# Steps 12 to 15 of a fused attention and network kernel worked in pairs, and two loads moved from one queue to another

## The chip, the cores and the metric

The kernel runs on one core of a Trainium2 chip. The metric is the device time of one execution in microseconds (us): the median over several runs. A core has four compute engines that the text names as the profile does: PE (the tensor engine: matmuls and transposes; its weight loads are shown apart as PEld), DVE (vector), ACT (scalar) and POOL (GpSimd). SP only issues transfers. All five take their instructions strictly in the order in which they were written for them, and wait for one another by semaphores. SBUF is the on-chip memory, PSUM the eight banks into which PE writes its results.

## The reference

```python
# attention, 4 batches x 8 heads, 768 positions, head size 64
k_sum = blocks of 32 keys, largest;  v_sum = blocks of 32 values, mean
scores_l = scale * q @ k.T, kept where |i - j| < 16
scores_s = scale * q @ k_sum.T + log(32)
a = softmax of [scores_l, scores_s];  attn = a @ [v, v_sum]
# network on the 3072 tokens, d_model 512, d_ff 1024
x = attn, heads side by side
out = (((x @ w1) * (x @ w2)) @ w3) @ w_out
```

## The kernel before, in words

**Work.** The 3072 tokens are six units of 512 (`U`), the eight heads four pairs of heads (`NPAIR`). One attention *step* is one unit and one pair: 24 steps, numbered unit by unit, so that steps 12 to 15 are the unit 3. A step has three pieces on PE: the scores (`scores`, L376, 32 small matmuls into two banks of the four called `sc`), the transposes of the softmax (`transposes`, L434, 16 into two banks) and the outputs (`outputs`, L457, 32 into one bank). Between them DVE takes minima and subtracts (`reduce`, L390), ACT exponentiates (`expose`, L404), ACT and DVE invert, ACT normalizes (`normalize`, L414), ACT, or ACT and DVE, copy the transposes out (`evacuate`, L442 to L446), and ACT copies the outputs (`keep_raw`, L477).

The network takes nearly all of PE. Weights and activations are held as a high and a low part, so each product is three matmuls of 512 columns. `w3` is first folded into `w_out` (`fold_weights`), then units 0 and 1 go the plain way (`gate`, `project`, all at L125), and units 2 with 3 and 4 with 5 go as two large products of seven partial products each (`lanes`, L740; the weights of the seven are sums that were stored to DRAM and are loaded back as `ws`). The first large product needs all outputs of units 2 and 3, that is of steps 8 to 15; its operands `xT` are made from them by `moving_x`.

**The written order.** The order on PE is written by hand. The network's matmuls are a generator, `stream`; `run(columns)` takes matmuls from it until so many columns have been given, and between two such runs the attention pieces are placed. A matmul is 512 columns, and `FAST` is 12288 columns, 24 matmuls, one partial product over four lanes. In FASTs, the fold ends at 8, the plain unit 0 at 20, the plain unit 1 at 32 (this point is `CLASSIC`), and the start of the large products follows there; `TO_SLOTS`, where the steps from 8 on begin, is 19.52. I call each place where attention pieces stand in the stream an *interruption*.

**Single steps.** Steps 8 to 15 (up to `SINGLE`, four units of four) are placed by `lump` (L1293): transposes of step p-2 and scores of step p, then 18 matmuls, then outputs of step p-2, then matmuls up to `UP_TO[p]`, 1.56 FAST a step. Each lump also loads and reduces two pieces of the later batches (`load_batch`, `reduce_batch`: block maxima of keys and means of values), and `EXTRA` hangs other work on a lump.

**Pairs of steps.** From step 16 on `two_steps` (L1331) places two at a time: the outputs of the pair before last and the scores of this pair, half a `LEAD` of 18 matmuls twice, then the rest of the period given by `BEGINS`, and in its middle the transposes of the pair before (`turn`). The first pair (m = 8) has to finish the single steps 14 and 15. In the written order ACT and DVE follow the same calls (`tc.manual_schedule(engines=VECTOR)`), while copies of the network float between them by priority. `LATER` hangs loads and the making of `xT` on a pair.

**Queues.** POOL's instructions are in written order too: it copies the block maxima into k (`gather`, L363) and issues the transfers of `load_values` (v, L325) from unit 4 on and of `load_scores` (q, L341, and k, L343) from step 18 on. SP issues the rest: v, q and k of earlier steps, the means (`fetch_means`, L359), the weight sums `wS<-sp` (L685) and their way back `ws<-wS` (L785), and the four loads of each of the two joined output weights (`load_joined`, L949, the transfer at L959: `wr<-pR`, 1 MB each half). SP's order past TO_SLOTS is chosen by the scheduler. The tiles `sp` and `ws` come from one set of six buffers, tag `x`, given out in turn; so do q and k (two each), v (two) and the tag `pt` (four, for the copies g and o of the plain units and for the first joined half).

**Banks.** Accumulators of the plain units take two `mm` banks, and every third of unit 1 takes one of the `sc` banks (`bank`, L492).

## Time and profile before

| | |
|---|---|
| runs | 507.43, 504.39, 507.6 us; median 507.43 |
| the profiled execution | 508.66 us, its span 506.9 us |
| PE busy in the span | 483.1 us, 95% |
| DVE, ACT, POOL busy | 357.0, 316.6, 66.5 us |
| granted clock of PE | 1.000 |

The span runs from the first to the last instruction; 1.76 us of the profiled execution lie around it. A line of a group names the source line, the engine, the operation, the tiles written and read, and the count; after the bar its busy time, the mean time of one in ns, and the idle time of the engine ahead of it with what ended it. In a chain of waits each line is a start, a length and what held the end back at that time. "xN" counts instructions. Matmuls overlap, so that one that lasts 390 ns is followed by the next after some 227 ns.

### The profile page before, as it was taken

What the parts mean: (1) busy time and instruction counts of PE and PEld (TensorE: products, weight loads), DVE (VectorE), ACT (ScalarE), POOL (GpSimd) and SP (SyncE); (2) the same over time, 40 slices, a digit from 0 to 9 for tenths busy, and PEclk for the clock granted to TensorE, in tenths of its full rate; (3) what the DMA queues carried; (4) which work ended last, traced back from release to release, by engine and by line L of the source; (5) the groups of instructions that cost most, each with busy time, mean ns of one, the idle gap of its engine ahead of it and who ended that gap; (6) DMA issues with size and microseconds to landing.
All of it is one profiled execution on the core that took longest, in us unless ns stands there. A gap on an engine that the chain in (4) does not pass through costs nothing.

```text
span 506.9 us, 10543 instructions
## 1 busy us (share of the span) xinstructions
PE 483.1 (95%) x3804; PEld 391.0 (77%) x3804; DVE 357.0 (70%) x873; ACT 316.6 (62%) x882; POOL 66.5 (13%) x121
## 2 busy tenths in 40 slices
PE   0889999999999999999997999999999999999997
PEld 0667777788877877777776888878888888888886
DVE  4978886897704888985657895799968029129972
ACT  5589964677716878878894868579634421523710
POOL 1024523000212110100221132112000000000000
PEclk9999999999999999999999999999999999999999
DMA  8998596999499999889999989998868765656762
GB/s 341 410 411 286 209 357 235 372 400 411 148 301 273 264 277 286 256 261 329 343 311 305 331 286 344 316 300 246 233 183 281 227 191 190 203 178 197 212 193 93
DMA packets 56068, 139.29 MB, mean 275 GB/s; under 512 B 6224, under 2 KB 19280, under 8 KB 53456
## 3 DMA queue, kind: packets, MB, share of 16 engines
q1 hardware_dynamic: 51600, 127.44, 74.5%
q0 software_dynamic: 3264, 9.08, 7.3%
q10 hardware_dynamic: 1152, 2.10, 1.1%
q8 instruction: 30, 0.49, 0.4%
q14 instruction: 22, 0.18, 0.1%
HBM read 105.89 MB, written 32.70 MB: 273 GB/s over the span
## 4 chain that ended last, share of the span: by engine, by line
PE 73%; DMA 13%; DVE 6%; ACT 5%; issue 1%; SPq 1%; POOL 0%; POOLq 0%; DVEq 0%; ACTq 0%
PE ln L740 39%; PE mm L125 25%; PE sc L376 4%; PE po L457 3%; DMA k<-in_kW_dram 3%; DMA ws<-wS 3%; DMA v<-in_vW_dram 2%; DMA wS<-sp 2%; PE tp L434 2%; ACT sm L404 2%; DVE w L121 2%; DVE wf L206 1%; DMA vS<-vs 1%; DMA wraw<-in_w_dram 1%; ACT w L220 1%; DMA wraw<-in_wo_dram 1%
## 5 line engine op out<-in xcount | busy, mean ns | idle before, releaser
L740 PE MATMUL ln<-xT,ws 128*128 128x512 f32 x672 | 155.6, 391 | 3.2 <-DMA ws<-wS 3.2
L740 PEld LDWEIGHTS ln<-xT,ws 128*128 128x128 f32 x672 | 125.4, 188 | 30.4 <-DVE xT L121 3.5
L125 PE MATMUL mm<-x,w 128*128 128x512 f32 x384 | 90.8, 394 | 0.2 <-DVE g L531 0.2
L125 PEld LDWEIGHTS mm<-x,w 128*128 128x128 f32 x384 | 71.1, 188 | 16.4 <-issue 0.8
L404 ACT ACTIVATE sm<-sm,mx 128x120 f32<-128x120 f32 x192 | 73.6, 387 | 13.3 <-DVE mx L390 13.1
L740 PE MATMUL ln<-hT,ws 128*128 128x512 f32 (+1 forms) x348 | 77.3, 383 | 0.0
L760 DVE TENSOR_TENSOR tmp<-ln,tmp 128x512 f32<-128x512 f32 (+1 forms) x53 | 35.6, 678 | 54.1 <-PE ln L740 39.3
L740 PEld LDWEIGHTS ln<-hT,ws 128*128 128x128 f32 x348 | 63.7, 188 | 12.8
L125 PE MATMUL mm<-w,w 128*128 128x512 f32 x192 | 49.9, 409 | 15.1 <-ACT w L220 12.5
L643 ACT CAST hT<-hr 128x512 fp32r<-128x512 f32 x56 | 32.1, 628 | 39.3 <-DVE hr L817 30.5
L125 PEld LDWEIGHTS mm<-w,w 128*128 128x128 f32 x192 | 36.0, 193 | 25.9 <-ACT w L220 13.2
L390 DVE CUSTOM_DVE_ANT_0 sm<-sc,mask_sb 128x120 f32<-128x120 f32 x192 | 41.3, 276 | 15.9 <-PE sc L376 15.9
L125 PE MATMUL mm<-wp,h 128*128 128x512 f32 x192 | 46.3, 395 | 0.0
L125 PEld LDWEIGHTS mm<-wp,h 128*128 128x128 f32 x192 | 35.4, 188 | 8.4 <-issue 0.5
L414 ACT ACTIVATE sm<-sm,mx 128x120 f32<-128x120 f32 x128 | 38.8, 388 | 3.1 <-DVE mx L410 2.4
L121 DVE TENSOR_TENSOR hT<-hr,hT 128x512 fp32r<-128x512 f32 x56 | 35.7, 688 | 3.1 <-ACT hT L643 3.0
L404 ACT ACTIVATION_READ_ACCUMULATOR sm<-sm,mx 128x1 f32 x192 | 36.6, 190 | 0.0
L363 POOL COPY k<-ks 128x96 f32<-128x96 f32 (+1 forms) x32 | 14.8, 476 | 157.0 <-DMA k<-in_kW_dram 140.6
L121 DVE TENSOR_TENSOR w<-wf,w 128x1024 fp32r<-128x1024 f32 (+1 forms) x22 | 25.6, 1167 | 8.2 <-ACT w L220 8.2
L220 ACT CAST w<-wf 128x1024 fp32r<-128x1024 f32 (+1 forms) x22 | 21.3, 969 | 14.5 <-DVE wf L206 13.2
L176 ACT ACTIVATE wf<-wraw 128x1024 f32<-128x1024 f32 (+1 forms) x22 | 23.1, 1061 | 7.4 <-DMA wraw<-in_wo_dram 3.8
L376 PE MATMUL sc<-k,q 64*64 64x120 f32 x768 | 25.4, 268 | 1.6 <-issue 0.8
(72 smaller groups left out, 564.0 us busy)
## 6 DMA issues: line engine op xcount, KB each, us to landing
ws<-wS SPq DMA_DIRECT2D x56, 512.0 KB
wraw<-in_w3T_dram SPq DMA_DIRECT2D x8, 1024.0 KB
wraw<-in_w_dram SPq DMA_DIRECT2D x8, 1024.0 KB
wS<-sp SPq DMA_DIRECT2D x16, 512.0 KB
ws<-pS SPq DMA_DIRECT2D x16, 512.0 KB
raw<-in_kT_dram SPq DMA_DIRECT2D x16, 392.0 KB
wS<-w SPq DMA_DIRECT2D x12, 512.0 KB
ws<-pW SPq DMA_DIRECT2D x24, 256.0 KB
```

Source lines behind the costliest of these rows:

```text
L121: eng.tensor_tensor(dst, src, hi.bitcast(F32), ALU.subtract)
L125: nc.tensor.matmul(acc, lhsT=a, rhs=b, start=first and i == 0, stop=last and i == len(terms) - 1)
L176: nc.scalar.activation(f[:, some], words[:, some, 1].bitcast(F32), AF.Prelu, scale=2.0**-112, alpha=-(2.0**32),)
L220: nc.scalar.copy(t[:, 0, some], f[:, some])
L376: nc.tensor.matmul(sc[h][64 * g : 64 * g + 64, i * KR : (i + 1) * KR], lhsT=q[rows, i * P + 64 * g : i * P + 64 * g + 64], rhs=k[rows, i, ...
L390: nc.vector.tensor_tensor_reduce(out=sm[:, j], in0=sc[h][:, i * KR : (i + 1) * KR], in1=mask_sb[:, 0 if blk == 0 else 2 if blk == BLOCKS - ...
L404: nc.scalar.activation(sm[:, j], sm[:, j], AF.Exp, bias=mx[:, 0, j : j + 1], scale=-1.0, accum_out=mx[:, 1, j : j + 1])
L414: nc.scalar.activation(sm[:, j], sm[:, j], AF.Copy, scale=mx[:, 2, j : j + 1])
L457: nc.tensor.matmul(po[cols, at : at + 64], lhsT=v[:KR, g, i, cols], rhs=pt[g][:, (h * NBLK + i) * 64 : (h * NBLK + i + 1) * 64], start=Tru ...
L643: nc.scalar.copy(dst[0], src)
L740: nc.tensor.matmul(bank[:, cols], lhsT=x, rhs=y[:, cols], start=c + j == 0 and (split or k in o.first), stop=c == steps - 1 and j == 2 and ...
L760: nc.vector.tensor_tensor(parts[to][:, cols], got, parts[more][:, cols], ALU.add)
```

## The change

Eight things change. (1) `LAST_UNITS` goes from 4 to 3, so single steps end with step 11 and pairs begin with m = 6; steps 12 to 15 are the pairs m = 6 and 7. `BEGINS` gets two entries more and a new third: the pairs begin at 25.3, 28.1, 31, 36, 40, 43.7, 46.2 and 50.6 FAST, and the four single steps left have 1.445 FAST each. (2) What the first pair had to do for the single steps is now done at m = 6 for steps 10 and 11. (3) Pairs 6 and 7 (`ahead`) also reduce and load the later batches, twice each, and pair 7 copies the second halves of its transposes out on DVE. (4) In the pair m = 8 (`BLOCKED`) the outputs of steps 14 and 15 aren't left to the next pair: they are placed at 33.4 FAST (`LAST_OUTPUTS`), the transposes before them at 32.4; their v is fetched at the pair's start. (5) Work of `EXTRA` for lumps 13 to 15 goes to `LATER` of pairs 7 and 8. (6) From the first pair on, the accumulators of unit 1 alternate between `mm` and `tp`. (7) v of steps 12 to 15 and q and k of steps 13 to 17 are issued by POOL and not by SP, as the two conditions hang on `LAST_UNITS`. (8) The joined weights are issued by POOL, the first half at the end of pair 8 (before: its beginning), the second at the end of pair 9 (before: the end of pair 8).

```diff
@@ -337,7 +337,7 @@
 
         q = sb.tile([P, U], F32, name="q")
         k = sb.tile([P, NBLK, COLS], F32, name="k")
-        eng = nc.gpsimd if u > LAST_UNITS or u == LAST_UNITS and p > 1 else nc.sync
+        eng = nc.gpsimd if u > LAST_UNITS or u == LAST_UNITS and p > 0 else nc.sync
         eng.dma_start(q, qG[p, :, u * U : (u + 1) * U])
         if u:
             eng.dma_start(k, kW[p, :, u * NBLK : (u + 1) * NBLK])
@@ -487,13 +487,14 @@
     made, pair_of_h = [0], [None]
     GATES = ("w1", "w2")
 
-    taken = [0]
+    taken, by_twos = [0], [False]
 
     def bank(wide):
 
 
         taken[0] += 1
-        return {"tag": "sc", "bufs": 4} if wide and taken[0] % 3 == 0 else {"tag": "mm", "bufs": 2}
+        third = {"tag": "tp", "bufs": 2} if by_twos[0] else {"tag": "sc", "bufs": 4}
+        return third if wide and taken[0] % (2 if by_twos[0] else 3) == 0 else {"tag": "mm", "bufs": 2}
 
     def gate(fs, x, hs, wide=False):
 
@@ -559,7 +560,7 @@
     NSU = NU // 2
     NS = NU * NPAIR
     NFIRST = 2 * NPAIR
-    LAST_UNITS = 4
+    LAST_UNITS = 3
     ALL_FOLD = 3 * DO * NJ * NF
     UNIT = 3 * (2 * U * NC * NF + DO * NF * NBLK)
     TO_SLOTS = ALL_FOLD + 0.96 * UNIT
@@ -956,7 +957,7 @@
         for h in range(2):
             for i in range(2):
                 to = t[i][h].rearrange("p (j d) -> p j d", d=DH)
-                nc.sync.dma_start(to, pR[c][:, h, :, i * DH : (i + 1) * DH])
+                nc.gpsimd.dma_start(to, pR[c][:, h, :, i * DH : (i + 1) * DH])
         joined[c] = t
 
     def sums_of_output(c):
@@ -1256,25 +1257,27 @@
     CLASSIC = ALL_FOLD + 2 * UNIT
     FAST = 3 * U * 4 * KH
     SINGLE = LAST_UNITS * NPAIR
-    UP_TO = {p: TO_SLOTS + (CLASSIC - TO_SLOTS) * (p - NFIRST + 1) / NFIRST for p in range(NFIRST, SINGLE)}
+    BLOCKED = (NU - 2) * NPAIR // 2
+    PAIRS = range(SINGLE // 2, NS // 2)
+    BEGINS = (-6.7, -3.9, -1, 4, 8, 11.7, 14.2, 18.6)
+    LAST_OUTPUTS = 1.4
+
+    def begins(m):
+        return CLASSIC + BEGINS[m - PAIRS[0]] * FAST if m - PAIRS[0] < len(BEGINS) else float("inf")
+
+    STEP = (begins(PAIRS[0]) - TO_SLOTS) / (SINGLE - NFIRST)
+    UP_TO = {p: TO_SLOTS + STEP * (p - NFIRST + 1) for p in range(NFIRST, SINGLE)}
     UP_TO[NFIRST] = ALL_FOLD + UNIT + 3 * U
     LEAD = 18 * U
-    PAIRS = range(SINGLE // 2, NS // 2)
-    LAST_SINGLE = 1.6
-    BEGINS = (0, 4, 8, 11.7, 14.2, 18.6)
-
-    def begins(m):
-        return CLASSIC + BEGINS[m - PAIRS[0]] * FAST if m - PAIRS[0] < len(BEGINS) else float("inf")
 
     VECTOR = {engines.Activation, engines.DVE}
-    EXTRA = {
-        13: [lambda: moving_x(1, 0), lambda: moving_x(1, 1)],
-        14: [lambda: gates_flow(1)],
-        15: [lambda: flow_in(4), lambda: moving_x(1, 2)],
-    }
+    EXTRA = {}
     LATER = {
-        (PAIRS[0], 0): [lambda: load_joined(0)],
-        (PAIRS[0], 1): [lambda: load_joined(1), *(lambda k=k: moving_x(1, k) for k in range(3, NK))],
+        (BLOCKED - 1, 0): [lambda: moving_x(1, 0), lambda: moving_x(1, 1)],
+        (BLOCKED - 1, 1): [lambda: gates_flow(1)],
+        (BLOCKED, 0): [lambda: flow_in(4), lambda: moving_x(1, 2)],
+        (BLOCKED, 1): [*(lambda k=k: moving_x(1, k) for k in range(3, NK)), lambda: load_joined(0)],
+        (BLOCKED + 1, 1): [lambda: load_joined(1)],
     }
 
     for i in range(NF):
@@ -1331,13 +1334,14 @@
     def two_steps(m):
 
         a, b = 2 * m, 2 * m + 1
-        first = m == PAIRS[0]
+        first, ahead = m == PAIRS[0], m < BLOCKED
         if first:
             fetch_means(*place(a - 1), values[a - 1])
         with tc.manual_schedule(engines=VECTOR):
             if first:
                 t, home = sms.pop(a - 2)
                 pt = evacuate(transposes(t), "A", home)
+                by_twos[0] = True
             for p in (a - 4, b - 4):
                 if p in turned:
                     finish_step(p, turned.pop(p), **SPARE)
@@ -1348,6 +1352,10 @@
                 reduce(u, 1, sc, sm, mx)
         if not first:
             fetch_values(a - 2)
+        if m == BLOCKED:
+            fetch_values(b - 2)
+            for p in (a - 2, b - 2):
+                fetch_means(*place(p), values[p])
         for work in LATER.get((m, 0), ()):
             work()
         if m in PAIRS:
@@ -1365,32 +1373,43 @@
                 expose(0, sm2, mx2)
                 reduce(u2, 1, sc2, sm2, mx2)
                 normalize(sm, mx)
-            if not first:
+                if ahead:
+                    reduce_batch()
+            if ahead:
+                load_batch()
+            if not first and m != BLOCKED:
                 fetch_values(b - 2)
             fetch(b + 2)
-            run(CLASSIC + LAST_SINGLE * FAST if first else (given[0] + begins(m + 1)) / 2)
+            run(CLASSIC + (begins(m + 1) - CLASSIC) * 0.1 if m == BLOCKED else (given[0] + begins(m + 1)) / 2)
             with tc.manual_schedule(engines=VECTOR):
-                if first:
-                    finish_step(a - 1, turned.pop(a - 1), **SPARE)
                 expose(1, sm2, mx2)
                 invert(mx2)
                 normalize(sm2, mx2)
-                if m - 1 - PAIRS[0] in joined:
-                    sums = sums_of_output(m - 1 - PAIRS[0])
+                if m - 1 - BLOCKED in joined:
+                    sums = sums_of_output(m - 1 - BLOCKED)
                     for _ in range(6):
                         next(sums)
                     background.append(sums)
+                if ahead:
+                    reduce_batch()
+            if ahead:
+                load_batch()
         if not first and m - 1 <= PAIRS[-1]:
             with tc.manual_schedule(engines=VECTOR):
-                turn((a - 2, b - 2), "A")
+                turn((a - 2, b - 2), "V" if ahead else "A")
         if m not in PAIRS:
             fetch_values(b - 2)
         for p in (a, b):
             fill(p + 2)
-            if not first and p - 2 in values:
+            if not first and m != BLOCKED and p - 2 in values:
                 fetch_means(*place(p - 2), values[p - 2])
         for work in LATER.get((m, 1), ()):
             work()
+        if m == BLOCKED:
+            run(CLASSIC + LAST_OUTPUTS * FAST)
+            with tc.manual_schedule(engines=VECTOR):
+                for p in (a - 2, b - 2):
+                    finish_step(p, turned.pop(p), **SPARE)
         run(begins(m + 1))
 
     with tensor_order, tc.manual_schedule(engines={engines.Pool}):
```

## The prediction

> **What bounds the kernel now.** I read the page's engine rows, then who PE waited for, then the chain of waits around steps 9 to 18.

> ```profile
> span 506.9 us, 10543 instructions
> PE 483.1 (95%) x3804; PEld 391.0 (77%) x3804; DVE 357.0 (70%) x873; ACT 316.6 (62%) x882; POOL 66.5 (13%) x121
> ```

> PE is the bound. Its waits, longest in total first:

> ```profile
> PE mm L125 <- ACT w L220: 12.5, 3, 11.5
> PE ln L740 <- DMA ws<-wS: 3.2, 1, 3.2
> ...
> PE sc L376 <- issue: 0.8, 2, 0.6
> PE sc L376 <- POOL k L363: 0.6, 1, 0.6
> ```

> The 12.5 us are the start, which the change doesn't touch. Past it PE stood still once for long: 3.2 us, for a weight sum `ws`. All else that can be won is inside PE's stream: what interruptions cost.

> ```profile
> 220.72 0.61 PE tp L434 x16
> 221.33 0.98 PE sc L376 x32
> 222.31 4.35 PE mm L125 x18
> 226.66 1.08 PE po L457 x32
> ...
> 274.77 1.80 PE sc L376 x64
> ...
> 317.12 1.09 PE tp L434 x32
> ...
> 326.63 2.02 PE po L457 x64
> 328.65 1.18 PE sc L376 x38
> 329.83 0.60 issue
> 330.43 0.98 PE sc L376 x26
> ...
> 349.69 24.07 PE ln L740 x105
> ```

> The first four lines are a single step, the others pieces of paired steps. Two stretches of matmuls give slope and offset: (24.07 - 4.35) / (105 - 18) = 0.227 us a matmul, and 4.35 - 18 x 0.227 = 0.27 us that each stretch costs besides, so each interruption costs 0.27 us for leaving and entering the stream.

> **The change part by part.** Sums are made against the profiled execution, 508.66 us (span 506.9).

> *Fewer interruptions.* From lump 12 to the middle of pair 9 there were 13: two in each of four lumps, three in pair 8 (transposes 14 with scores; outputs 14 with transposes 15; outputs 15), two in pair 9. Now there are 9: two in pair 6, two in pair 7, three in pair 8, two in pair 9. Four fewer: 4 x 0.27 = 1.08 us.

> *Pieces side by side.* Twice two single transposes become a double one (2 x 0.61 - 1.09 = 0.13), twice two scores (2 x 0.98 - 1.80 = 0.16), twice two outputs (2 x 1.08 - 2.02 = 0.14): 2 x 0.43 = 0.86 us.

> *A wait that comes in.* Where outputs stand ahead of four scores, six `sc` banks are wanted and four are there, so the second step's scores wait for ACT's copy of an output. The rows at 328.65 show it: 1.18 + 0.60 + 0.98 = 2.76 us against 1.80, so 0.96. Pair 8 newly has two outputs ahead of its scores: +0.96. Pair 7 has one, for which no row stands; between 0 and 0.96, near 0, since one copy has the 0.98 us of step 14's scores to run beside: +0.2. The wait of scores for POOL's `k` (0.6) stood at pair 8, whose second step is fetched late; step 13 is fetched in the same late way by lump 11, so it moves and stays. Net so far: -1.08 - 0.86 + 1.16 = -0.8.

> *The 3.2 us.* What stood behind the late `ws`:

> ```profile
> 254.71 10.22 DMA wS<-sp
> 264.95 3.96 DMA ws<-wS
> ```

> The store of a sum took 10.22 us, and its buffer was the one that the next `ws` had to have. Around it SP issued the joined weights, and the DMA engines were full (view of the transfers, 245 to 265 us):

> ```profile
> 249.05 1.15 SPq L959 DMA_DIRECT2D wr<-pR  x2
> ...
> 252.51 0.36 SPq L959 DMA_DIRECT2D wr<-pR  x1
> ...
> 253.50 0.89 SPq L959 DMA_DIRECT2D wr<-pR  x2
> 254.71 0.33 SPq L685 DMA_DIRECT2D wS<-sp  x1
> 256.20 0.98 SPq L959 DMA_DIRECT2D wr<-pR  x2
> ```
> ```profile
> DMA  9999999999999999999999999999999999999643
> ...
> DMA packets 3959, 6.60 MB, mean 330 GB/s; under 512 B 420, under 2 KB 2802, under 8 KB 3956
> ...
> wr<-pR SPq DMA_DIRECT2D x8, 256.0 KB
> ```

> Of 6.60 MB in these 20 us, 2 MB were the joined weights, in small pieces. The change takes half of them a whole pair later and moves the other half behind POOL's fills of pair 8, onto another queue. About a third of the traffic goes or thins, and 30 transfers in all leave SP (12 of v, 10 of q and k, 8 `wr`). A store that lands 3.2 us sooner in 10.22 is within that. I take the whole 3.2 off; bounds 0 (the store stays as late) and 3.2. A second candidate ends at the same place: a weight load is put down to `xT`, made from step 15's output.

> ```profile
>   DVE xT L121: 3.5, 1
>   DMA ws<-wS: 3.2, 1
> ```

> Outputs 14 and 15 now come 36 matmuls past CLASSIC, and product 3, which needs both, still begins at matmul 72; before, output 15 came at 39. So this one gains 3 matmuls, 0.7 us, unless ACT is late, which is the next term.

> [...]

> *ACT in pairs 6 to 8.* ACT's busy time in the five stretches from 185 to 243, one step each, and in pair 8, with its groups between 185 and 243:

> ```profile
> sum 57.99, PE 57.99 PEld 46.04 DVE 46.13 ACT 47.16 POOL 2.37; mean PE 11.60 PEld 9.21 DVE 9.23 ACT 9.43 POOL 0.47
> ```
> ```profile
> 243.31:258.13 14.82, 14.71 (x201) 11.93 (x200) 9.13 (x43) 13.73 (x47) 6.32 (x13) 1.00 1.05 356
> ```
> ```profile
> L404 ACT ACTIVATE sm<-sm,mx 128x120 f32<-128x120 f32 x40 | 15.4, 388 | 1.6 <-DVE mx L390 1.6
> L414 ACT ACTIVATE sm<-sm,mx 128x120 f32<-128x120 f32 x42 | 12.7, 382 | 2.5 <-DVE mx L410 1.8 <-DMA q<-in_qG_dram 0.7
> ...
> L442 ACT COPY sm<-tp 120x512 f32<-120x512 f32 x5 | 2.8, 564 | 0.0
> ```

> So 9.43 of 11.60 a step. Pair 6 lasts 2.8 FAST, 67 x 0.227 = 15.2, plus about 4.7 of pieces, 19.9 us, for 2 x 9.43 = 18.9 of ACT: 95%, where it was 81%. It fits, just. Then pair 8. Its outputs 14 and 15 come 19.9 us after its begin (pieces 4.8, 36 matmuls 8.2, transposes 1.1, 24 matmuls 5.4, two entries 0.5). ACT can start exponents about 3.3 us in (outputs 2.02, the first scores 0.98, a first minimum). Before those outputs it must do 16 exponents (16 x 0.385 = 6.2), 16 normalizations (16 x 0.30 = 4.8), inversions 0.4 and the four copies of transposes 14 and 15, which the written order puts behind step 17's normalization (4 x 0.56 = 2.2), and the network's copies: a step has 9.43, of which the same attention work takes 7.0 (half of the above, and an output copy), so 2.4 in 11.6 us or some 4 in 19.9. That ends at 20.9: +1.0. Bounds: 0, and the lag that ACT already showed in old pair 8:

> ```profile
> 257.04 1.15 PE L457 MATMUL po<-sm,v 120*64 120x64 f32 x32
> ```
> ```profile
> 260.91 0.59 ACT L477 COPY xraw<-po 128x512 f32<-128x512 f32 x1
> ```

> Output 15 ended at 258.19 and its copy began at 260.91, 2.7 late; so 0 to 2.7.

> *Parts at nothing.* Accumulators between `mm` and `tp`: PE shows no wait for those copies there; if it came, 0.2 us as the one wait on `g` in the table. DVE's batches in pairs 6 and 7: DVE 9.23 of 11.60 a step, and PE needs the banks only 18 matmuls (4.1 us) later. The moved `xT` work keeps its place in columns. POOL takes 30 issues more.

> ```profile
> k<-in_kW_dram POOLq DMA_DIRECT2D x6, 368.0 KB, 9.7
> ...
> v<-in_vW_dram POOLq DMA_DIRECT2D x8, 192.0 KB, 6.8
> ```
> ```profile
> 255.94 1.52 POOL L325 DMA_DIRECT2D v<-in_vW_dram  x3
> ```
> ```profile
> SPq L959 <- DMA out_dram<-o: 1.8, 1, 1.8
> ```

> At half a us each (1.52 / 3) that is 16 us on an engine busy 13%. They are hidden by the pair's 20 us against 6.8 to 9.7 us of landing; only v of steps 14 and 15 has less: asked for when outputs 12 and 13 end (some 1 and 2 us in), landed by 12, needed at 19.9. The joined load now waits in POOL's order for `pt` buffers (SP waited 1.8 for the same), and behind it stand v of 16 and 17, q and k of 20 and 21 and their fills, needed a pair later: nothing.

> **The sum.** -0.8 - 3.2 + 1.0 = -3.0: the profiled execution would take 505.7. It lies 1.2 above the median of the runs, 507.43; the same step from the median gives 504.4, which I forecast. That one of the three runs took 504.39, 3.0 less, suits a wait that isn't in every execution.

> **The rivals.**

> *The store stays late* (chance 0.2). `ws`, `sp` and half of the joined weights still meet on full DMA engines, and the wait stays or shows at the next `ws`. For it: nine tenths busy in nearly every slice above. Against: 1 MB less at that time. 507.43 - 0.8 + 1.0 = 507.6.

> *All covers hold* (0.13). Neither ACT nor banks make PE wait: 507.43 - 1.94 - 3.2 = 502.3, and 502 where the wait for `k` goes too.

> *ACT becomes the bound of pairs 6 to 8, slower than before* (0.12). At 95% by an estimate, ACT lags where copies of the network and of sums bunch. Its order is fixed, so the lag is paid wherever PE needs a copy out of a bank: outputs 12 and 13, outputs 14 and 15, then product 3. At 2.7 each that is 8.1, with the store's wait hidden in it: 507.43 - 0.8 - 3.2 + 8.1 = 511.5. It decides from 4.0 us in all (0.8 + 3.2). For it: 13.73 of 14.82 busy in pair 8. Against: DVE takes half the copies in pair 7, and later pairs show no such wait.

> *POOL brings v of 14 and 15 late* (0.05). From landing 8 us before it is due to past it: two v in one stretch of a full ring, 3 us beyond due: 504.4 + 3 = 507.4. [...]

> **How the numbers follow.** The forecast has 0.5, its own range 502.5 to 506.5 (copies of ACT 0 to 2.7, pair 7's banks 0 to 0.96). The range for 8 in 10 takes in late stores, v and good covers, and ACT's rival in its lower half: 500.0 to 510.0. A measurement of this kernel can tell about 1%, 5.1 us, from no change: faster than 502.4 is most of the good covers and a fifth of the forecast's share, 0.22; slower than 512.5 is the upper part of ACT's rival and what I haven't seen, 0.12; between, 0.66.

> **What would show it.** Right: nine interruptions from pair 6 on; no wait of PE on `ws<-wS` above 0.5 us near the third partial product; the store of that sum in 6 to 7 us; scores of 16 and 17 in some 2.7; outputs 14 and 15 held by ACT about 1 us. Wrong: a row of PE waiting on DMA as long as before, or PE waiting on ACT's copies for over 4 us between pairs 6 and 9, or on POOL.

## The result, and the profile after

| | before | after |
|---|---|---|
| median of 14 runs each, us | 508.24 (504.39 to 512.73) | 511.40 (509.72 to 514.06) |
| the profiled execution, us | 508.66, span 506.9 | 512.62, span 510.9 |

The ratio of after to before is 1.0083, 95% interval 1.0056 to 1.011: the change makes the kernel slower by 0.8%. That is 7.0 us above my forecast, and outside its range of 500.0 to 510.0. The ratios, here and below, are taken from the undisturbed runs alone and aren't the quotient of the two medians (1.0062); one run of a_spread, 803.76 us at a granted clock of 0.56, stands in its median and not in its ratio.

The page of after, its head and engine rows:

```profile
span 510.9 us, 10545 instructions
PE 484.2 (95%) x3804; PEld 393.4 (77%) x3804; DVE 357.2 (70%) x873; ACT 317.4 (62%) x882; POOL 78.6 (15%) x151
```

The work is the same; POOL has the 30 issues more. Who PE waited for (total us, times, longest):

```profile
PE mm L125 <- ACT w L220: 11.9, 2, 11.4
PE sc L376 <- ACT xraw L477: 5.8, 1, 5.8
...
PE ln L741 <- DMA ws<-wS: 1.9, 1, 1.9
PE mm L125 <- ACT sm L442: 0.6, 1, 0.6
```

The start (the first row) is as before. The second row is new and is the result: a single wait of 5.8 us, of scores for ACT's copy of an output. The one wait on `ws` is shorter than the 3.2 us of before, and stands elsewhere.

*The account.* I compare PE's stream from the first double transposes, at about 127 us, to the start of the last stretch, which lasts 127.6 us in every kernel. Each stretch of n matmuls is priced at 0.227 n + 0.27 us and each attention piece as in the prediction (0.61, 0.98, 1.08; 1.09, 1.80, 2.02 in pairs). What is left over is PE waiting or running at a lower clock; I call it the *excess*. It is that of one profiled execution of each kernel.

| us | before | after | difference |
|---|---|---|---|
| the region | 247.87 | 252.80 | +4.93 |
| stretches x 0.27 | 27 | 23 | -1.08 |
| attention pieces | 49.29 | 48.43 | -0.86 |
| excess | 5.62 | 12.49 | +6.87 |

In before the excess is 3.39 for the late `ws` at 268.8, 0.95 and 0.88 in the scores of pairs 11 and 10, for which the profile names no cause, 0.34 for `k`, and small things. In after it is 7.07 in the scores of step 15 at 215, 0.87 in the stretch behind them, 2.18 at 319.9 for a `ws`, 0.94 in the scores of pair 10, 0.86 at 197.5 and small things. So the saving by structure came, and the excess took 3.5 times as much.

*The 7.07 us.* The chain of waits of after, from the load that starts it to PE (start, length, what):

```profile
198.76 10.19 DMA raw<-in_kT_dram
...
209.04 0.95 DVE ks L266
209.99 0.60 DVE h L121
...
215.10 0.70 DVE g L532
...
215.82 0.63 ACT h L533
...
217.16 0.15 DVE mx L410
...
217.34 0.40 ACT sm L414
217.73 0.47 ACT g L526
218.20 2.01 ACT sm L414 x7
220.21 1.03 ACT sp L680 x2
221.24 0.52 ACT h L533
221.76 0.49 ACT xraw L477
...
222.29 1.87 PE sc L376 x30
```

A load of keys of a later batch, asked for at 198.76, lands at 209.0. DVE comes to its reduction (`ks`, L266) long before and stands. Behind it, in DVE's written order, wait its parts of the network and the reciprocal `mx` of step 13; ACT can't normalize step 13 (`sm`, L414) without that, and the copy of step 11's output (`xraw`, L477) stands behind this normalization in ACT's written order. The copy frees the `sc` bank that the second half of step 15's scores needs. PE, which has nothing to do with the load, stands from 216.5 to 222.3.

DVE's waits of after between 190 and 260 us, and two rows of its timeline (start, length, operation; in brackets the idle time ahead):

```profile
DVE ks L266 <- DMA raw<-in_kT_dram: 4.6, 2, 3.7
...
DVE vs L283 <- DMA raw<-in_vB_dram: 2.9, 1, 2.9
```
```profile
203.77 0.95 DVE L266 TENSOR_REDUCE ks<-raw 128x24 f32<-128x768 f32 x1 [0.85 <-DMA raw<-in_kT_dram]
...
209.04 0.95 DVE L266 TENSOR_REDUCE ks<-raw 128x24 f32<-128x768 f32 x1 [3.72 <-DMA raw<-in_kT_dram]
```

Before, DVE waited for no such load after 190 us. The tile `raw` in both kernels between 180 and 262 (270) us says why: the third column of numbers is the first and the last start of the four loads of keys (L261) and of their four reductions (L266). Before:

```profile
L261 SPq DMA_DIRECT2D raw<-in_kT_dram x4: 357/357/357, 199.3 to 211.7; - x4
L266 DVE TENSOR_REDUCE ks<-raw x4: 900/922/948, 209.3 to 221.8; 128x24 f32<-128x768 f32 x4
```

After:

```profile
L261 SPq DMA_DIRECT2D raw<-in_kT_dram x4: 328/344/1257, 196.2 to 210.0; - x4
L266 DVE TENSOR_REDUCE ks<-raw x4: 911/948/954, 203.8 to 218.0; 128x24 f32<-128x768 f32 x4
```

A lump asked, and reduced one lump later: 10.0 us from issue to use for the first and 10.1 for the last. In the pair it is reduced one part of the period later: 7.6 and 8.0 us, and for the first two of the four DVE had been standing. Without its 0.85 and 3.72 us of standing it came to them 6.7 and 6.6 us after their issue.

The loads themselves grew as well. The trace records each update of a transfer's semaphore, and by the last of them these two loads took 7.45 and 10.19 us in after, where the same two took 3.02 and 3.35 us in before: 6.6 us would have been enough for those. The DMA engines are fuller around them (before, then after; the next to last number is the DMA share):

```profile
199.30:202.30 3.00, 3.00 (x15) 2.43 (x14) 3.00 (x10) 2.60 (x8) 0.00 (x0) 1.00 0.56 158
```
```profile
196.20:203.70 7.50, 6.89 (x70) 5.29 (x70) 6.20 (x39) 7.06 (x32) 1.80 (x4) 1.00 0.95 304
```

In after POOL issues q and k of two steps beside them, 1.25 MB between 195.8 and 197.7 us; in before SP issues its q and k behind them, at 202 and 203. That this slows the loads is likely; a_queues_back, below, bears it out for some 3 of the 10.2 us.

*What was forecast for pairs 8 and 9* (the chain of after):

```profile
242.26 2.01 PE po L457 x64
244.27 1.80 PE sc L376 x64
...
261.25 2.02 PE po L457 x64
```

Pair 8 has two outputs ahead of its scores and no wait for a bank (1.80 is the price without one), and outputs 14 and 15 take their 2.02 without ACT holding them.

### The profile page after: what moved, and what is told of

It reads as the page before. It is cut to its first block, busy times and chain, and to the rows that moved or that the text cites. A ratio compares the mean times of both kernels' runs of the same rounds, so it can differ in the third digit from the quotient of the medians.

```text
span 510.9 us, 10545 instructions
## 1 busy us (share of the span) xinstructions
PE 484.2 (95%) x3804; PEld 393.4 (77%) x3804; DVE 357.2 (70%) x873; ACT 317.4 (62%) x882; POOL 78.6 (15%) x151
## 4 chain that ended last, share of the span: by engine, by line
PE 65%; ACT 13%; DVE 10%; DMA 9%; issue 1%; SPq 0%; ACTq 0%; DVEq 0%
PE ln L741 36%; PE mm L125 23%; DMA ws<-wS 4%; ACT sm L404 3%; PE po L457 3%; PE sc L376 2%; DMA raw<-in_kT_dram 2%; DMA wS<-sp 2%; DVE wf L206 2%; ACT w L220 2%; ACT sm L414 1%; DVE w L121 1%; ACT wf L176 1%; PE tp L434 1%; ACT hT L644 1%
## 5 line engine op out<-in xcount | busy, mean ns | idle before, releaser
L125 PE MATMUL mm<-x,w 128*128 128x512 f32 x384 | 90.5, 394 | 0.6 <-ACT sm L442 0.6
L125 PEld LDWEIGHTS mm<-x,w 128*128 128x128 f32 x384 | 71.2, 188 | 16.7 <-ACT sm L442 1.1
L404 ACT ACTIVATE sm<-sm,mx 128x120 f32<-128x120 f32 x192 | 73.5, 386 | 10.8 <-DVE mx L390 10.6
L125 PE MATMUL mm<-w,w 128*128 128x512 f32 x192 | 51.0, 418 | 13.9 <-ACT w L220 11.9
L125 PEld LDWEIGHTS mm<-w,w 128*128 128x128 f32 x192 | 36.9, 198 | 24.9 <-ACT w L220 12.1
L390 DVE CUSTOM_DVE_ANT_0 sm<-sc,mask_sb 128x120 f32<-128x120 f32 x192 | 41.1, 276 | 15.6 <-PE sc L376 15.6
L125 PE MATMUL mm<-wp,h 128*128 128x512 f32 x192 | 46.6, 399 | 0.0
L125 PEld LDWEIGHTS mm<-wp,h 128*128 128x128 f32 x192 | 36.3, 192 | 8.6 <-issue 0.6
L414 ACT ACTIVATE sm<-sm,mx 128x120 f32<-128x120 f32 x128 | 39.2, 386 | 2.5 <-DVE mx L410 2.5
L121 DVE TENSOR_TENSOR hT<-hr,hT 128x512 fp32r<-128x512 f32 x56 | 35.6, 684 | 3.1 <-ACT hT L644 3.0
L404 ACT ACTIVATION_READ_ACCUMULATOR sm<-sm,mx 128x1 f32 x192 | 36.6, 190 | 0.0
L376 PE MATMUL sc<-k,q 64*64 64x120 f32 x768 | 25.6, 273 | 6.2 <-ACT xraw L477 5.8
L121 DVE TENSOR_TENSOR w<-wf,w 128x1024 fp32r<-128x1024 f32 (+1 forms) x22 | 25.6, 1165 | 8.2 <-ACT w L220 8.2
L220 ACT CAST w<-wf 128x1024 fp32r<-128x1024 f32 (+1 forms) x22 | 21.4, 971 | 14.8 <-DVE wf L206 13.5
L376 PEld LDWEIGHTS sc<-k,q 64*64 64x64 f32 x768 | 21.0, 136 | 9.0 <-ACT xraw L477 6.3
## 6 DMA issues: line engine op xcount, KB each, us to landing
ws<-pW SPq DMA_DIRECT2D x24, 256.0 KB
```

The lines of the kernel that those rows point to most:

```text
L121: eng.tensor_tensor(dst, src, hi.bitcast(F32), ALU.subtract)
L125: nc.tensor.matmul(acc, lhsT=a, rhs=b, start=first and i == 0, stop=last and i == len(terms) - 1)
L220: nc.scalar.copy(t[:, 0, some], f[:, some])
L376: nc.tensor.matmul(sc[h][64 * g : 64 * g + 64, i * KR : (i + 1) * KR], lhsT=q[rows, i * P + 64 * g : i * P + 64 * g + 64], rhs=k[rows, i, ...
L390: nc.vector.tensor_tensor_reduce(out=sm[:, j], in0=sc[h][:, i * KR : (i + 1) * KR], in1=mask_sb[:, 0 if blk == 0 else 2 if blk == BLOCKS - ...
L404: nc.scalar.activation(sm[:, j], sm[:, j], AF.Exp, bias=mx[:, 0, j : j + 1], scale=-1.0, accum_out=mx[:, 1, j : j + 1])
```

## The experiments

**The theories.** The first: DVE's written order, with a load that needs up to 10 us and has some 7, costs what after lost (a later reduction gives it back). The rivals: v, q and k moved from SP to POOL make the loads late (moving them back gives it back); the joined weights on POOL bring a late sum (moving them alone costs); ACT is too full in pairs 6 to 8 (nothing but less work on ACT helps). All ratios are to before, measured beside the same chip's runs of it (medians 507.30, 508.26 and 508.24 in the three groups); the excess is that of the profiled execution, which can lie 2 to 3 us off the median (508.51 in a_late_finish, 514.42 in a_spread_sp, 503.00 in a_spread_nofinish), so that single numbers of that column compare roughly.

| kernel | median us | ratio, 95% | excess |
|---|---|---|---|
| a_late_reduce | 508.24 | 1.0013 (0.9979 to 1.0047) | 6.61 |
| a_queues_back | 511.76 | 1.0085 (1.0054 to 1.0117) | 10.63 |
| b_joined_late | 508.76 | 1.0014 (0.9986 to 1.0043) | 5.92 |
| b_queues_pool | 506.25 | 0.9979 (0.9950 to 1.0007) | 5.73 |
| a_late_finish | 510.68 | 1.0036 (1.0002 to 1.0070) | 8.06 |
| a_later_finish | 508.32 | 0.9996 (0.9963 to 1.0030) | 6.26 |
| a_later_finish_joined | 508.01 | 0.9980 (0.9946 to 1.0014) | 6.94 |
| b_both_queues | 507.50 | 0.9980 (0.9948 to 1.0012) | 5.85 |
| a_no_load_wait | 514.90 | 1.0129 (1.0073 to 1.0186) | 13.56 |
| a_spread | 506.01 | 0.9969 (0.9935 to 1.0003) | 3.61 |
| a_spread_sp | 511.25 | 1.0052 (1.0014 to 1.0090) | 13.83 |
| a_spread_nofinish | 504.97 | 0.9957 (0.9920 to 0.9993) | 2.70 |

**a_late_reduce: the reductions half a pair later.** After, with the batches reduced in the middle of pair 6, twice in pair 7 and once in the first half of pair 8.

```diff
-                if ahead:
+                if not first and m <= BLOCKED:
                     reduce_batch()
-            if ahead:
+            if not first and ahead:
                 load_batch()
```

> The changed kernel, with DVE's work on the later batches half a pair later: none in the first half of pair 6, one in its second half, two in pair 7, one in pair 8; each load follows its reduction as before, so a load has some 10 us in place of 5 before DVE needs it. Theory 1 (the wait of the scores of step 15, 6.1 us, begins at DVE, whose written order puts the block maxima ahead of what ACT needs, while the keys are still on their way): DVE's 4.6 us of waiting on raw go, PE's wait on the output copy falls below 1 us, and the time is 504 to 506, 5 to 7 below the changed kernel's 511.4. Theory 2 (ACT itself is overloaded in pairs 6 and 7): the wait stays at 5 us or more, 510 to 512. Theory 3 (the loads are late because q, k and v moved to POOL's queue and bunch there): between, 507 to 509, since the late transfers hit the next user.

508.24 us: about 3.5 us of the loss are back (ratio to before 1.0013 where after had 1.0083). PE's wait in step 15's scores, and DVE's waits between 190 and 260:

```profile
PE sc L376 <- ACT xraw L477: 1.5, 1, 1.5
```
```profile
DVE vs L283 <- DMA raw<-in_vB_dram: 4.0, 1, 4.0
```

DVE no longer waits for keys, and the wait in the scores of step 15 falls from 5.8 to 1.5. The 1.5 that stay are ACT's: step 13 is normalized ahead of the copy. The wait of DVE has gone to the last load, of values; next to it PE stands 1.2 us ahead of outputs 12. The first theory holds for the place and for 5.1 of the 7.07 us there. The time gives back 3.5 us where I expected 5 to 7, and lies where I had put the third theory (507 to 509); a_queues_back and a_spread tell the two apart.

**a_queues_back: v, q and k of these steps on SP again.** After, with

```diff
-            (nc.gpsimd if u >= LAST_UNITS else nc.sync).dma_start(v[rows, g], vW[u, p, rows, g])
+            (nc.gpsimd if u >= 4 else nc.sync).dma_start(v[rows, g], vW[u, p, rows, g])
...
-        eng = nc.gpsimd if u > LAST_UNITS or u == LAST_UNITS and p > 0 else nc.sync
+        eng = nc.gpsimd if u > 4 or u == 4 and p > 1 else nc.sync
```

> The changed kernel with v of steps 12 to 15 and q and k of steps 13 to 17 issued by SP again; all else as changed. Theory 1: the keys are still needed 5 us after their load is asked for, DVE still waits 3 us or more on raw and PE 4 us or more on the output copy; 510 to 512. Theory 3: DVE's wait on raw goes and the time is 504 to 506.

511.76 us, what after took (1.0085 against 1.0083). Moving the queue back gives nothing back in sum. Inside it things moved, DVE's wait for keys here and in after being 1.6 and 4.6 us:

```profile
DVE ks L266 <- DMA raw<-in_kT_dram: 1.6, 1, 1.6
```

I had expected 3 us or more. The second load of keys took 7.26 us here and 10.19 in after, DVE waited 3.0 less, and step 15's scores lost 4.10 and not 7.07, which is 2.97 less: one for one, as the first theory has it. So the third theory holds in part: the issue from POOL makes these keys some 3 us later (9.92 and 7.46 us in a_spread and a_spread_sp). But 2.27 came at 267.9 (matmuls waiting for ACT's copy `hr`) and 1.74 in the scores of pair 10, and the sum stays.

**b_joined_late: the joined weights alone.** Before, with

```diff
-                nc.sync.dma_start(to, pR[c][:, h, :, i * DH : (i + 1) * DH])
+                nc.gpsimd.dma_start(to, pR[c][:, h, :, i * DH : (i + 1) * DH])
...
-        (PAIRS[0], 0): [lambda: load_joined(0)],
-        (PAIRS[0], 1): [lambda: load_joined(1), *(lambda k=k: moving_x(1, k) for k in range(3, NK))],
+        (PAIRS[0], 1): [*(lambda k=k: moving_x(1, k) for k in range(3, NK)), lambda: load_joined(0)],
+        (PAIRS[0] + 1, 1): [lambda: load_joined(1)],
```

> The kernel before with one part alone: the joined weights issued by POOL, the first half at the end of pair 8, the second at the end of pair 9. The prediction's step (the 3.2 us wait on a weight sum comes from these loads on SP): PE's wait on ws falls below 0.5 us near the fourth partial product, 505 against 508.2. Rival (the wait belongs to the six shared buffers or comes from the operand xT and moves on): a wait on ws of 2 us or more is found again there or at a later product, 507.5 to 509.

508.76 us, no difference that can be told. The wait at 268.8 is gone, and nothing ahead of it delays PE here; by its semaphore the store that took 10.22 us in before takes 5.80. So the joined weights did hold that store, as the prediction had it. But the chain now shows the same thing a partial product later:

```profile
289.85 9.03 DMA wS<-sp
...
298.94 15.43 DMA ws<-wS
...
314.51 2.36 PE ln L740 x6
```

The excess there is 3.76, and 0.75 in the transposes behind it. After shows this wait too, in the chain of waits:

```profile
295.37 9.97 DMA wS<-sp
...
305.40 14.58 DMA ws<-wS
...
320.11 1.60 PE ln L741 x6
```

These loads of `ws` take 14.58 and 15.43 us. The joined pieces were issued ahead of them in both kernels, from 256.7 to 296.7 and 297.5 us, but they aren't needed for it: in before, where no joined piece is issued past 257.2, the same load is issued at 301.47 and takes 12.67 us. It lands there at 314.14, some 1.6 us ahead of PE. In b_joined_late it lands at 314.37, hardly later, and PE, which now comes to it 4 us sooner, waits.

**b_queues_pool: v, q and k alone.** Before, with the two conditions as after has them (`u >= 3`; `u > 3 or u == 3 and p > 0`).

> The kernel before with one part alone: v of steps 12 to 15 and q and k of steps 13 to 17 issued by POOL. Theory 3: DVE begins to wait on raw and PE on ACT's copies between 195 and 245 us, 510 to 513. Theory 1: a lump leaves each load 10 us, no such wait, 507 to 509; SP's relief alone may take up to 3.2 off if the wait on a weight sum comes from SP's crowding, 505.

506.25 us, unclear against no difference. No wait for a `ws` is left, for two reasons. The store that took 10.22 us in before takes 6.76 here (255.26 to 262.02 by its semaphore), with the joined weights where they were, so v, q and k had their part in holding it. And PE now waits 2.2 us for the copy of transposes ahead of an output, at 214, and runs at half clock behind (0.50 granted from 217.60 to 221.01), 3.7 us together, so that it comes 3.7 us later to the product that had waited 3.4.

```profile
PE po L457 <- ACT sm L442: 2.2, 1, 2.2
```

**b_both_queues: both queue moves on before.**

> The kernel before with both moves between queues (q, k and v of steps 12 to 17 and the joined weights, late), single steps as before. From the two alone: the wait on a weight sum at 268 is gone, and one of 2 to 3 us stands near 314, after the second joined half; 507.5 to 509. If the forecast's view of the joined weights were right after all, no wait on ws anywhere: 504 to 505.

507.50 us, again no difference. Nothing at 214, nothing at 268.8 (that store takes 3.89 us), and 3.24 at 314.8 with 0.78 behind it; the next load of `ws` lands at 314.94. Four kernels with the single steps of before (before itself and these three) have an excess of 5.62, 5.92, 5.73 and 5.85. A wait of some 3 us is taken away each time and comes back at another place.

**a_late_finish: also the outputs of step 11 earlier.** a_late_reduce with the outputs of step 11, whose copy held the bank, in the middle of pair 6:

```diff
             with tc.manual_schedule(engines=VECTOR):
+                if first:
+                    finish_step(a - 1, turned.pop(a - 1), **SPARE)
                 expose(1, sm2, mx2)
```

> The run with the late reductions, and the outputs of step 11 placed in the middle of pair 6 (as the kernel before does with step 15 in its first pair) and not at the head of pair 7: one interruption more (0.27 us). What was left there was 1.95 us of PE waiting, in the scores of step 15, for ACT's copy of output 11, which stands in ACT's order behind the normalization of step 13. Theory 1b (the written order of ACT, with an output ahead of four scores, holds the rest): that wait goes, 1.5 us less than the run with late reductions, about 506.5. Theory 2 (ACT overloaded): the wait stays or moves to the outputs of step 12, 508 to 509.

510.68 us, a miss of 4. The wait in step 15's scores is gone to nothing, and 4.94 us stand in outputs 12 and 13 instead: DVE waits 4.2 us for a load of values and copies its half of the transposes late.

```profile
PE po L457 <- DVE sm L446: 3.2, 1, 3.2
```

**a_later_finish and a_later_finish_joined: later still.** Reductions in the middle of pair 6, the first half of pair 7, the first half of pair 8 and after outputs 14 and 15; in the second kernel the joined weights are on SP again too, their second half at the beginning of pair 9.

> As the one with step 11 finished early, and the reductions of the later batches spread further: the middle of pair 6, the first half of pair 7, the first half of pair 8, and after outputs 14 and 15, so that each load has 10 us or more. Theory 1: DVE's wait of 4.0 us on the blocks of values and with it PE's 1.2 us at the outputs of step 12 go too; 505 to 505.5. Theory 2: no change against the one with step 11 early.

> The one before in this list, with the joined weights issued by SP again, the first half at the end of pair 8, the second at the beginning of pair 9 (SP's scheduler places both near 255 us). If the joined halves themselves make a weight sum late wherever they land: the wait on ws stands near 268 us, 2 to 3 us, 506 to 508. If only the second half at the end of pair 9 did harm: no wait on ws at 268 nor at 318, 504 to 505.

508.32 and 508.01 us; the first is 3 more than I expected. In the first the last two loads are asked for at 243.5 and 245.3 and take 8.2 and 7.9 us; DVE comes to them at 245.5, some 8 us before PE makes the outputs 14 and 15 behind which I had written them, and waits 6.2 us (7.0 in the second). ACT stands 3.5 us for a reciprocal behind them, and PE loses 3.8 us between 257 and 268. So the 10 us that I expected weren't given, and moving the wait moved the cost. In the second kernel no wait on `ws` stands near 268 or 318, but neither does one in the first, so this doesn't tell what the joined weights do.

**a_no_load_wait: no wait for the last batch at all.** After, with the last batch's keys and values brought to a place in DRAM that nothing reads, and its reductions reading the tile of an earlier load. It leaves out the right maxima and means of that batch.

```diff
+    def keys_aside(p):
+        nc.sync.dma_start(aside[p], kT[B - 1, p])
+    def old_keys(p):
+        summaries(B - 1, p, last[0].rearrange("p a b -> p (a b)")[:, : PAD + S])
...
+            if b == B - 1:
+                blocks = [(lambda c=c: blocks_aside(c), lambda raw, c=c: value_means(B - 1, c, last[0])) for c in range(vB.shape[1])]
+                rows_of_keys = [(lambda p=p: keys_aside(p), lambda raw, p=p: old_keys(p)) for p in range(NPAIR)]
```

> The changed kernel, in which DVE never has to wait for keys and values of the last batch: their loads go to a place aside in DRAM, with the same bytes on the same queue, and the reductions stand where they stood but read the last values of the batch before. It leaves out the right maxima and means of the last batch; the amount of work is the same. Theory 1 (DVE's written order waits for the keys): no wait of DVE on raw, the 7.1 us in the scores of step 15, the 0.9 of halved clock behind them and the 0.9 before them go, all but up to 2 us that ACT's order may keep; 503 to 506 against 511.4. Theory 2 (ACT overloaded): 4 us or more of waiting on ACT's copies stay, 509 or more.

514.90 us: the total says nothing, since another thing came in. Free of buffers, the copies went earlier in SP's order (one at 178.5 took 9.4 us), and stores of sums came late beside them, which holds ACT:

```profile
ACT sp L680 <- DMA wS<-sp: 8.6, 3, 5.8
```

That is 7.5 us of excess between 184 and 201. What it does tell: with no DVE wait for `raw`, step 15's scores lose 2.08 and not 7.07, as in a_late_reduce. So about 5 us of the 7.07 are the keys, and 2 are ACT's order. PE comes there late by the 7.5 us, so this run alone wouldn't show it; a_late_reduce (1.95) and a_spread_nofinish (1.66) agree.

**a_spread, a_spread_nofinish: the reductions spread further.** After, with the reductions in the middle of pair 6 and in the first halves of pairs 7, 8 and 9; the first kernel has the earlier outputs of step 11 besides.

```diff
-                if ahead:
+                if not first and m <= BLOCKED + 1:
                     reduce_batch()
-            if ahead:
+            if not first and m <= BLOCKED + 1:
                 load_batch()
...
-                if ahead:
+                if first:
                     reduce_batch()
-            if ahead:
+            if first:
                 load_batch()
```

> The whole computation: outputs of step 11 in the middle of pair 6, reductions of the later batches in the middle of pair 6 and in the first halves of pairs 7, 8 and 9, so that every load has half a pair or more (12 us at least). Theory 1: no wait of DVE on raw above 1 us; the sum of PE's waits from lump 8 on falls from 12.5 us (changed kernel) and 5.6 (before) to 2 to 3, so 503.5 to 505.5, below both kernels. Theory 2: waits on ACT's copies of 2 us or more stay; 506.5 to 509.

> The spread reductions with the output of step 11 at the head of pair 7, as changed: PE waits 1.5 to 2 us in the scores of step 15 for ACT's copy behind the normalization of step 13 (theory 1b), less 0.27 for one interruption fewer: 1 to 2 us slower than with step 11 early. If ACT's lag in the late runs came from DVE alone: 0.3 us faster.

506.01 and 504.97 us; the two can't be told apart, where I expected the second 1 to 2 us slower; the second is faster than before, its interval just clear of 1 (as the fastest of nine variants of after it may owe some of its 0.4% to chance). The page of a_spread_nofinish, PE's waits past 126 us, and its tile `raw` from 180 to 300:

```profile
span 501.2 us, 10545 instructions
PE 481.7 (96%) x3804; PEld 391.7 (78%) x3804; DVE 356.7 (71%) x873; ACT 317.5 (63%) x882; POOL 79.3 (16%) x151
```
```profile
PE sc L376 <- ACT xraw L477: 1.3, 1, 1.3
```
```profile
...
L261 SPq DMA_DIRECT2D raw<-in_kT_dram x4: 333/346/1627, 195.0 to 214.1; - x4
L266 DVE TENSOR_REDUCE ks<-raw x4: 902/927/944, 212.3 to 224.0; 128x24 f32<-128x768 f32 x4
```

The first load of keys has 17.3 us, where DVE came to it after 6.7 in after, and DVE waits for none. The loads are no faster (6.3 and 10.1 us for the first two). The two later ones didn't get the 12 us that I meant, but 9.9 (7.6 in a_spread), and landed in 3.4 and 4.7. PE waits once, 1.3 us, for ACT's order. The region is 243.01 us: against before's 247.87 that is -4.86, of which -1.94 is the structure and -2.92 the excess (2.70 against 5.62). Against after it is -9.79, all of it excess. The profiled executions exaggerate this: their spans are 9.7 us apart, the medians 6.4.

**a_spread_sp: a_spread with v, q and k on SP.** The two conditions as in a_queues_back.

> The one before, with v of steps 12 to 15 and q and k of steps 13 to 17 issued by SP again. If the move to POOL relieved SP: 1 to 4 us slower than it, with a wait on ws or on ACT's copies near 260 us; if not, within 1 us of it.

511.25 us, 5.2 more than a_spread. In the profile 5.88 of the excess are at 319, with matmuls at half clock (the longest with `ws` took 793 ns where the median is 389; the mean granted clock of that execution is 0.993), and 2.58 at 264.6:

```profile
PE ln L741 <- DMA ws<-wS: 4.4, 1, 4.4
```

Once the reductions have time, the move to POOL is worth about 1% here, by these two kernels alone. On after the same edit changed nothing in sum (a_queues_back): it won 3 us at the keys and lost 4 us later.

## Why the prediction was wrong, point by point

- **Fewer interruptions, pieces side by side: right.** Four stretches fewer, and pieces of pairs at 2.01, 1.80 and 2.02 in the rows above: -1.94 by the prices put on them.
- **DVE's batches in pairs 6 and 7, put "at nothing": this is the step that failed.** I priced them by DVE's share, "9.23 of 11.60 a step", and by PE needing the banks "only 18 matmuls (4.1 us) later". Neither asks when the load that the reduction reads will be there. The busy share held (DVE 15.0 of the 20.4 us of pair 6), and DVE stood 4.6 + 2.9 = 7.5 us between 190 and 260 with work behind it: the way from issue to use went from 10.0 to 6.6 us, and the loads of keys from 3.0 and 3.4 us to 7.5 and 10.2. The 4.6 us for keys cost about 5 of the 7.07 us, and the 0.87 behind them.
- **The bank wait of pair 7, +0.2, "near 0, since one copy has the 0.98 us of step 14's scores to run beside": wrong by the same thing.** It took the copy to start when the output ends. For pair 8 I had written out ACT's order ahead of the outputs; in pair 7 I didn't, though there the normalization of step 13 stands ahead of the copy of output 11. With the keys there in time this costs 1.66 (a_spread_nofinish) to 2.08 us. My upper bound of 0.96 was too low even for this part.
- **The bank wait of pair 8, +0.96: it didn't come** (1.80), and I had misread the row at 328.65. The timeline of before there (ACT's second copy, and where the scores go on):

```profile
328.69 0.58 ACT L477 COPY xraw<-po 128x512 f32<-128x512 f32 x1 [0.35 <-PE po L457]
...
330.43 0.98 PE L376 MATMUL sc<-k,q 64*64 64x120 f32 x26 [0.60 <-issue]
```

  ACT had copied both outputs by 329.27, before PE stopped at 329.83. The 0.60 was no wait for these copies, and the profile names none ("issue"); I made a rule of banks from it, where the row said that nothing was known.
- **The 3.2 us: the cause was right, and the wait wasn't won.** That store took 10.22 us in before, 6.76 with v, q and k moved alone, 5.80 with the joined weights moved alone, 3.89 with both and 4.01 in after, where I had said 6 to 7. But the load of the next product lands no sooner (314.14 in before, 314.37 in b_joined_late), and in after 2.18 us came back at 319.9, behind a store of 9.97 and a load of 14.58 us. Of the bounds 0 and 3.2 I took the wrong end; what I left out is the next load, though the rival of the late store named "the next `ws`". In after, PE comes 7 us late to the first product anyhow, so its missing wait at 268.8 can't be put down to the store alone.
- **ACT at outputs 14 and 15, +1.0: 0.** They took 2.02. ACT's copy of output 14 began at 264.2, 1.9 us after that output's end and 1.0 after both, and PE didn't wait for that bank.
- **Accumulators in `mm` and `tp`, "if it came, 0.2": it came, 0.86** at 197.5, where matmuls waited for the copy of transposes; a_queues_back has no such wait.
- **POOL's 30 issues: hidden, as said.** POOL is busy 78.6 us where it was 66.5: 0.40 us each. PE waits for no v, and the rival of the late v didn't come: the transfers of v that POOL issued in after between 207.4 and 263.7 landed in 2.9 to 9.2 us. No run shows the "full ring" of that rival or its 3 us. By a_spread and a_spread_sp (506.01 and 511.25 us) POOL is even the better issuer here.
- **The sum.** -1.94, -3.39 + 2.18 for `ws`, +7.07 + 0.87 for step 15 and the clock behind it, +0.86 for accumulators, and some -0.7 for the scores of pairs 8, 10 and 11 and small things: +4.93 in the region. Where the reductions have time, the sum of the prediction comes out: 504.97 measured, 504.4 forecast. That is luck in part, as the terms are others than mine (no ACT wait in pair 8, but one of 1.66 in pair 7).
- **The rival with the right time had the wrong mechanism.** "ACT becomes the bound of pairs 6 to 8", 511.5 us, hits 511.4 and even the name of the wait (PE for ACT's copies, over 4 us, as my sign of being wrong had it). But that is luck, since ACT wasn't full: between 213.7 and 217.3 it worked for little more than 1.2 us and stood for 2.2 us at one place, waiting for DVE. That DVE, in its written order, waits for a load was no rival of mine. By my own limits (502.4 and 512.5) the 511.4 lies "between", which had 0.66; the ACT rival had 0.12.

What stays open: what holds PE for 0.9 us in the scores of pair 10 in before, in after and in most of these runs; the profile names nothing. Three buffers for `raw` in place of two would let the loads be asked for earlier without moving the reductions; that wasn't tried on the chip. Why some executions differ by 3 us and more of one kernel isn't explained either: in one profile of a_late_reduce 4 us of it came ahead of 131 us, in code that is the same in all (PE stood 2.3 us for DVE's `g` at 89 us, and half clock followed; the mean granted clock of that execution is 0.996).

## What to carry to other kernels

When work that reads a transfer is moved into the written order of an engine, work out for every reduction the time from its load's issue to its turn and compare it with how long such loads take at that place beside the traffic there (here 7.5 and 10.2 us, at DMA shares of 0.95 and 0.88), not with how long they took before the change (3.0 and 3.4); the busy share of the engine says nothing on it. Then read what is written behind it, on that engine and on those that wait for it, to the first thing PE needs. A wait that is removed from a nearly full PE is won only if the next thing that PE comes to is earlier too: three ways of removing the 3.2 us changed the sum of waits by 0.1 to 0.3.

## What the runs showed of the hardware

```profile
215.86:219.27 3.41, 0.60 (x20) 0.37 (x10) 3.32 (x6) 3.14 (x10) 2.31 (x5) 1.00 0.54 169
219.27:222.68 3.41, 0.39 (x8) 0.39 (x12) 2.85 (x6) 3.38 (x9) 0.31 (x1) 0.50 0.90 314
222.68:226.10 3.42, 3.42 (x35) 2.73 (x28) 3.42 (x25) 2.22 (x12) 1.45 (x4) 0.50 1.01 283
```

The same in b_queues_pool, behind a stand of 2.2 us, and no half clock in before, where PE stood longer, 3.2 us from 265.9 to 269.1, but across such a point:

```profile
214.18:217.60 3.42, 1.22 (x33) 1.10 (x32) 2.45 (x18) 3.42 (x12) 0.00 (x0) 1.00 0.97 312
217.60:221.01 3.41, 3.41 (x14) 2.65 (x10) 3.38 (x7) 2.73 (x11) 2.64 (x5) 0.50 1.00 357
```
```profile
264.31:267.73 3.42, 1.59 (x8) 0.97 (x6) 3.42 (x8) 3.42 (x11) 0.00 (x0) 1.00 0.64 187
267.73:271.14 3.41, 2.09 (x9) 1.77 (x10) 1.10 (x3) 1.79 (x4) 0.00 (x0) 1.00 0.94 309
```

In these traces half clock went with how much of one such stretch PE stood. Between 30 and 500 us of the fourteen traces, half clock followed twelve stretches, in which PE stood 1.68 to 3.08 of the 3.41 us (2.20 in b_queues_pool, 2.81 and 3.02 in after); the longest stands in stretches that it didn't follow are 1.83 (before, at 264.31) and 1.85 us (after, at 318.26). My estimate from these numbers is that the line lies near half a stretch. Half clock lasted one stretch or two each time, 3.41 us in b_queues_pool and 6.83 in after, in which a matmul came every 427 ns and not 227, and cost some 0.7 to 1.5 us (0.75 in b_joined_late, 0.87 in after, 1.5 in b_queues_pool). PE needn't stand throughout such a stretch: in that of b_queues_pool it worked 1.22 of the 3.42 us.
